# Second-layer products split into fp32r parts from chunk 7 on, with the third split product in steps 3 and 5 of a chunk

## The chip, the core and the metric

The kernel runs on one core of a Trainium2 chip. The metric is the device time of one execution in microseconds (us); the kernel before takes 1778.03 us, the median of three runs (1777.51 to 1778.36).

## What is computed

A Fourier mixing layer is followed by a two-layer block with the hard-swish activation:

```python
X = np.fft.fft(np.fft.fft(x, axis=1), axis=2).real      # x: 8 x 3008 x 256
x = X.reshape(24064, 256)
h = x @ w_in                                            # 256 x 2048
g = h * np.clip(h + 3.0, 0.0, 6.0) / 6.0
out = g @ w_out                                         # 2048 x 256
```

Inputs and output are float32.

## The kernel before

**Tiling.** The batch is four pairs (NP = 4). The sequence transform of a pair has two stages: `stage1` (64-row tables on TensorE, L327, copied out by L339 and L340 and sent to DRAM) and `stage2` (L563), which gives the transposed columns of one chunk. A pair has 12 chunks (NCK), 48 in all, numbered by `n_all`; a chunk is 256 columns wide, the last of each pair (`ch.last`) 192. The feature transform is folded into the first layer's weights. A chunk goes through the two layers in 8 steps (`fc`), each with 256 of the 2048 hidden features.

**First layer.** A *unit* is 512 columns of one step's hidden features. Its sums are split products: KQ and KW hold three fp32r parts of the data and of the weights, and a product is three fp32r matmuls (`passes`, L717). Even and odd rows of the contraction come apart: `passes(nx, 0)` adds the even rows of the next unit onto a seed that ScalarE wrote (`seed`, L732 and L736, from the row QN), ScalarE copies the even sum out (`keep_even`, L741, tile s), `odd_half` adds the odd rows (the 127-row matmuls of L717) and takes a relu of the sum (L791, t from u), VectorE forms the other sign (`other_sign`, L751, v in the PSUM tile y0), ScalarE takes its relu (L791, t from v), and two `gates` on VectorE (L794) write the activation A.

**Second layer.** Each step is seven Strassen products per chunk (`mlp2`, L865), accumulated in PSUM over the 8 steps. `combine` on GpSimd (L809) forms the four mixed operands c a step ahead. A plain product is one fp32 matmul, which the profile shows as two rows of L865. A *split product* is three fp32r matmuls: a high part with the weight kept in GH, and two others with the weights in GK. From chunk CHUNK2 = 8 on, NFR = 2 products of every step are split: `split_gates` makes the high part of two operands on ScalarE (L886), copies it into a PSUM tile y1 or y0 (L891) and lets VectorE make the other two (L892, L893, tile J). In steps listed in THIRD = (4,) a third product is split by `split_third` (L900 and L903 on ScalarE, L904 and L905 on VectorE), whose copy always goes to y0.

**Weights.** `split_weights` (L914 to L919) makes the parts GK, one step's weights at a time; `keep_high` (L924, L926) replaces a step's GH by its high part once no unsplit product needs it, through a PSUM bank: two ScalarE instructions.

**Order.** Everything is in program order per engine. The main loop (from L1689) runs one *cycle* per unit: `odd_half`, one product, `other_sign`, one product, even passes of the next unit, gates, then `size - 2 - behind_it` products, the matmuls of a `stage1` if there is one, and `behind_it` products; then the next seed, the high parts of a following step (`flush(high_of)`), and `third_others`. The numbers of products in each cycle come from `place`: 6 or 7 per cycle. With `sizes = [6] * 7 + [7] * 2` a chunk has nine cycles, with `[7] * 8` it has eight. `third_high` starts a third product's high part in the middle of a cycle, one step ahead; `third_others` at a cycle's end makes the rest. I count cycles from 1; chunk 3 has cycles 3 to 11, chunk 5 cycles 21 to 29 before, and chunk 8 starts with cycle 48.

Of the kernel before, what the change touches and what calls it, by code (L numbers as in the profile page):

```python
# [7 lines left out]
F32 = mybir.dt.float32  # L8
# [52 lines left out]
def kernel(  # L61
# [66 lines left out]
    NSLOT, CHUNK1 = 9, 3  # L128
    CHUNK2, NFR = 8, 2
    THIRD = (4,)  # L130
    SPLIT = CHUNK1 * NF - 2
# [5 lines left out]
    F1 = consts.tile([P, 5 * PB], F32, name="F1")  # L137
    FI = consts.tile([P, NIX + 1 + P], F32, name="FI")
    IX = FI[:, 0:NIX].bitcast(I32)
# [4 lines left out]
    G = consts.tile([P, 6 - NFR, NF, P], F32, name="G")  # L144

    def split_products(fc):
        return NFR + (fc in THIRD)

    GH = [consts.tile([P, split_products(fc), P], F32, tag=f"GH{fc}", name="GH") for fc in range(NF)]
    G2 = {fc: consts.tile([P, P], F32, tag=f"G2{fc}", name="G2") for fc in range(NF) if fc not in THIRD}  # L150

    def weight(i, fc):
        if i == NFR and fc in G2:
            return G2[fc][:]
        return GH[fc][:, i] if i <= NFR else G[:, i - NFR - 1, fc]
    half = consts.tile([P, 1], F32, name="half")
# [673 lines left out]
    def split_of(ch, fc):  # L830
        return ch.n_all >= CHUNK2

    def order_of(ch, fc):

        if not split_of(ch, fc):
            return [[(i, None)] for i in range(7)]
        high, others = ([(i, j) for i in range(NFR)] for j in (HIGH, OTHERS))
        rest = [[(i, ALL if i < split_products(fc) else None)] for i in range(NFR, 7)]
        if ch.final and fc >= NF - LAST:
            return [high, others] + [rest[i - NFR] for i in (3, 5, 6, 4, 2)]  # L840
        if fc in THIRD:
            rest = rest[1:3] + rest[0:1] + rest[3:]
        order = [high] + rest[:2] + [others] + rest[2:]
        while len(order) > 7:
            order[0:2] = [order[0] + order[1]]
        return order

    def mlp2(ch, fc, lo, hi):
        a = ch.a[fc].rearrange("p m f n -> p (m f) n")[:, :, 0:ch.n]
        c = ch.c[fc]  # L850
        moving = [a[:, 0], a[:, 1], a[:, 3], c[:, 0], c[:, 1], c[:, 2], c[:, 3]]
        order = order_of(ch, fc)
        if fc == NF - 1 and lo == 0:
            ch.e = epool.tile([P, 5, TB], F32, tag="e", bufs=1, name="e")
            if ch.final:
                ch.e2 = epool.tile([P, 2, TB], F32, tag="s", bufs=1, name="e")
        for i, parts in (x for part in order[lo:hi] for x in part):
            if fc == 0 and i % 2 == 0 and parts != OTHERS:
                ch.acc[i // 2] = ps_a.tile([P, 2, TB], F32, tag="acc", name="acc")
            o = ch.acc[i // 2][:, i % 2, 0:ch.n]  # L860
            for j in parts or (None,):
                assert (j is None) != (weight(i, fc).dtype == F32R)
                w = weight(i, fc) if not j else GK[fc][:, j - 1, i]
                x = moving[i] if j is None else J3[:, j, 0:ch.n] if i == NFR else parts_tile(ch, fc)[:, j, i, 0:ch.n]
                nc.tensor.matmul(o, w, x,  # L865
                                 start=(fc == 0 and i % 2 == 0 and j in (None, 0)), stop=(fc == NF - 1),
                                 skip_group_check=True)
# [42 lines left out]
    def split_weights(fc):  # L910

        low, rest = (GK[fc][:, k] for k in range(2))
        ps = bank([P, split_products(fc), P], "high")
        nc.scalar.mul(low, GH[fc][:], HIGH_PART)  # L914
        nc.vector.tensor_scalar(ps[:], low.bitcast(F32), 1.0 / EPS, None, op0=AL.mult)
        nc.vector.scalar_tensor_tensor(low, GH[fc][:], (1.0 + EPS) / EPS, ps[:], op0=AL.mult, op1=AL.subtract)
        nc.vector.scalar_tensor_tensor(ps[:], ps[:], -EPS, low.bitcast(F32), op0=AL.mult, op1=AL.add)
        yield
        nc.vector.tensor_scalar(rest, ps[:], 1.0 / (1.0 + EPS), None, op0=AL.mult)  # L919

    def keep_high(fc):

        ps = bank([P, split_products(fc), P], "high")
        nc.scalar.copy(ps[:], GH[fc][:])  # L924
        GH[fc] = consts.tile([P, split_products(fc), P], F32R, tag=f"GH{fc}", name="GH")
        nc.scalar.mul(GH[fc][:], ps[:], HIGH_PART)  # L926
        yield

# [173 lines left out]
    def join(j):  # L1102
# [7 lines left out]

        outs = GH[2 * n + i][:, 0:NFR], G[:, B12 - NFR - 1:B22 - NFR:B22 - B12, 2 * n + i]
        for h, o in enumerate(outs):
# [3 lines left out]
    def mix_w_out(j):  # L1116

        g = {i: G[:, i - NFR - 1, 2 * j:2 * j + 2, :] for i in range(NFR + 1, 7)}
        tt = nc.gpsimd.tensor_tensor
# [4 lines left out]
        for k in range(2):  # L1124
            tt(weight(2, 2 * j + k), g[5][:, k], GH[2 * j + k][:, B21], op=AL.subtract)

# [30 lines left out]


    def load_table():
        nc.sync.dma_start(out=F1[:], in_=c_stage1[:, 8 * PB:13 * PB])  # L1160
# [14 lines left out]
    load_w(0, nc.sync)  # L1175
    nc.scalar.dma_start(out=F[:], in_=c_stage1[:, 0:8 * PB])
    nc.scalar.dma_start(out=FI[:], in_=c_stage1[:, 13 * PB:])
    zero = QN[PB:PX, 2]
# [125 lines left out]
    def beside():  # L1304
# [5 lines left out]
        for t, gr in ((2, 2), (10, 3)):  # L1310
            put(t, load_t, gr)
        put(2, spread_half, halves[0], 1)
        put(5, load_table)
        put(NF - 1, close_w)
# [40 lines left out]
    def open_slots():  # L1355
        nonlocal A, GK
# [3 lines left out]
        GK = [slots.tile([P, 2, split_products(fc), P], F32R, tag=f"GK{fc}", name="GK") for fc in range(NF)]  # L1360

# [4 lines left out]

    epool = jpool = KW = A = GK = J = J3 = None
    steps = [(p, ck, fc) for p in range(NP) for ck in range(NCK) for fc in range(NF)]
# [256 lines left out]
    seed(units[1])  # L1625
    weights_of, rested, kept = list(range(NF)), 0, 0

# [3 lines left out]

    thirds = [s for s in gates_of if steps[s][2] in THIRD]
    third = []

    def third_high():

        if thirds and not third and thirds[0] <= now[0] + 1:
            ch, fc = chunk(thirds.pop(0))
# [50 lines left out]
    while done < len(stream):  # L1689
# [18 lines left out]
        third_high()  # L1708
        if not un:
            third_others()  # L1710

# [56 lines left out]
        flush(high_of)  # L1768
        third_others()
        for gen in parts:  # L1770
            next(gen, None)
# [112 lines left out]
```

## Time and profile before

| | |
|---|---|
| median of 3 runs | 1778.03 us |
| profiled execution, its own time | 1779.34 us |
| its span, first to last instruction | 1777.5 us |
| granted TensorE clock, mean | 0.999 |
| PE busy | 1764.3 us (99%) |
| VectorE (DVE) busy | 1494.5 us (84%) |
| ScalarE (ACT) busy | 1411.4 us (79%) |
| GpSimd (POOL) busy | 1312.7 us (74%) |

An execution's time is its span and 1.8 us around it. A busy time is a union of the instructions' durations. Matmuls overlap in the pipeline, so their durations (376 ns for a row of an fp32 matmul of 256 columns) are longer than the distances of their starts; a pace is read from starts, best from one cycle's first 127-row matmul of L717 to the next cycle's.

### The profile page before, as it was taken

The page shows a single profiled execution, that of the slowest core. Times are in us where ns is not written, and L with a number is a line of the kernel's source. Part 1 is how long each engine was busy: PE and PEld are TensorE (multiplying, and loading weights), DVE is VectorE, ACT ScalarE, POOL GpSimd, SP SyncE. Part 2 cuts the span into 40 slices and gives each one's busy share as a digit, 9 for nine tenths or more (in the row PEclk, how much of TensorE's full clock was granted, in tenths as well). Part 3 has the DMA queues.
Part 4 walks back from the last instruction along what each step waited for, and adds up shares of the span by engine and source line. Part 5 has one row for each costly group of instructions (what it writes and reads, how often), then busy time and mean ns, then how long its engine had stood idle before and what let it go on. Part 6 is the DMA issues. An engine that isn't in the chain of part 4 may idle for free.

```text
span 1777.5 us, 30218 instructions
## 1 busy us (share of the span) xinstructions
PE 1764.3 (99%) x9632; PEld 1518.3 (85%) x9632; DVE 1494.5 (84%) x2868; ACT 1411.4 (79%) x2573; POOL 1312.7 (74%) x1474
## 2 busy tenths in 40 slices
PE   8999999999999999999999999999999999999998
PEld 6688888888988888888998888888899888888897
DVE  8988676668988888888898888888899888888887
ACT  6556666678888888888888888888888888888885
POOL 5687777776678787886768878887766766776675
PEclk9999999999999999999999999999999999999999
DMA  8433332312113222121112222321111111101101
GB/s 281 121 93 99 103 78 70 85 37 51 37 48 81 71 64 78 47 73 43 30 44 64 70 78 57 86 64 37 48 36 34 37 21 48 41 19 45 21 13 34
DMA packets 160811, 110.39 MB, mean 62 GB/s; under 512 B 122562, under 2 KB 141344, under 8 KB 160652
## 3 DMA queue, kind: packets, MB, share of 16 engines
q1 hardware_dynamic: 151900, 82.22, 18.5%
q0 software_dynamic: 7504, 25.65, 4.7%
q8 instruction: 76, 1.25, 0.3%
q14 instruction: 83, 0.68, 0.1%
q10 hardware_dynamic: 1248, 0.59, 0.1%
HBM read 71.93 MB, written 36.79 MB: 61 GB/s over the span
## 4 chain that ended last, share of the span: by engine, by line
PE 95%; DVE 2%; ACT 2%; issue 0%; DMA 0%; another core or an unknown queue 0%; DVEq 0%; ACTq 0%
PE acc L865 58%; PE u L717 27%; PE ps L563 2%; PE ps L327 2%; PE acc L819 1%; PE v L613 1%; PE u L613 1%; ACT t L791 1%; PE spare L1138 0%; DVE v L751 0%; PE ps L526 0%; PE ps L395 0%; PE awake L1165 0%; DVE J L892 0%; ACT PM L1069 0%
## 5 line engine op out<-in xcount | busy, mean ns | idle before, releaser
L865 PE MATMUL acc<-c,G 128*128 128x256 f32 (+1 forms) x3008 | 766.7, 376 | 0.0
L717 PE MATMUL u<-KQ,KW 128*128 128x512 f32 (+7 forms) x2376 | 743.8, 426 | 1.0 <-ACT s L741 0.6
L809 POOL TENSOR_TENSOR c<-A 128x512 f32<-128x512 f32 (+1 forms) x359 | 453.9, 1264 | 337.3 <-PE acc L865 328.5
L865 PEld LDWEIGHTS acc<-c,G 128*128 128x128 f32 x3008 | 533.1, 189 | 80.3 <-issue 12.8
L717 PEld LDWEIGHTS u<-KQ,KW 128*128 128x128 f32 (+1 forms) x2376 | 426.1, 189 | 67.0 <-ACT s L741 3.0
L791 ACT ACTIVATE t<-u,half 128x512 f32<-128x512 f32 (+1 forms) x384 | 261.9, 682 | 169.9 <-PE u L717 111.7
L791 ACT ACTIVATE t<-v,half 128x512 f32<-128x512 f32 (+1 forms) x384 | 262.3, 683 | 106.1 <-DVE v L751 104.5
L751 DVE SCALAR_TENSOR_TENSOR v<-s,u 128x512 f32<-128x512 f32 (+1 forms) x360 | 247.0, 686 | 117.5 <-ACT t L791 111.6
L809 POOL TENSOR_TENSOR c<-c,A 128x256 f32<-128x256 f32 (+1 forms) x359 | 260.4, 725 | 28.2
L809 POOL TENSOR_TENSOR c<-A,c 128x256 f32<-128x256 f32 (+1 forms) x359 | 260.2, 725 | 28.2
L794 DVE SCALAR_TENSOR_TENSOR A<-t,v 128x512 f32<-128x512 f32 (+3 forms) x481 | 250.2, 541 | 36.7 <-ACT t L791 34.1
L865 PE MATMUL acc<-J,GK 128*128 128x256 f32 (+1 forms) x1340 | 270.7, 322 | 1.4 <-DVE J L905 0.8
L892 DVE SCALAR_TENSOR_TENSOR J<-high,A 128x512 fp32r<-128x512 f32 (+1 forms) x315 | 211.2, 670 | 55.8 <-ACT high L891 45.4
L794 DVE SCALAR_TENSOR_TENSOR A<-t,u 128x512 f32<-128x512 f32 (+3 forms) x481 | 248.4, 537 | 0.0
L732 ACT ACTIVATE u<-QN,WN 128x512 f32<-128x512 f32 (+1 forms) x324 | 224.8, 694 | 0.0
L865 PEld LDWEIGHTS acc<-J,GK 128*128 128x128 f32 x1340 | 204.7, 189 | 17.5 <-DVE J L893 1.6
L893 DVE SCALAR_TENSOR_TENSOR J<-high,A 128x512 fp32r<-128x512 f32 (+1 forms) x315 | 210.5, 668 | 0.0
L886 ACT ACTIVATE J<-A 128x512 fp32r<-128x512 f32 (+1 forms) x315 | 193.4, 614 | 0.0
L891 ACT COPY high<-J 128x512 f32<-128x512 f32 (+1 forms) x315 | 185.2, 588 | 4.9 <-DVE KQ L893 2.4
L741 ACT COPY s<-u 128x512 f32<-128x512 f32 (+2 forms) x315 | 180.3, 572 | 9.5 <-PE u L717 8.3
L865 PE MATMUL acc<-A,G 128*128 128x256 f32 (+1 forms) x630 | 184.6, 375 | 0.0
L865 PEld LDWEIGHTS acc<-J,GH 128*128 128x128 f32 x670 | 125.8, 189 | 24.1
(184 smaller groups left out, 1808.5 us busy)
## 6 DMA issues: line engine op xcount, KB each, us to landing
out_dram<-o SPq DMA_DIRECT2D x744, 32.0 KB
T<-in_c_stage_dram SPq DMA_DIRECT2D x26, 512.0 KB
g<-zd SPq DMA_DIRECT2D x42, 256.0 KB
zd<-z SPq DMA_DIRECT2D x48, 192.0 KB
QN<-qd SPq DMA_DIRECT2D x43, 128.0 KB
xt<-in_x_dram SPq DMA_DIRECT2D x21, 256.0 KB
st<-in_moe_w_out_dram POOLq DMA_DIRECT2D x7, 512.0 KB
xt<-in_x_dram SPq DMA_DIRECT2D x17, 192.0 KB
```

The costliest lines, as they stand in the source:

```text
L717: nc.tensor.matmul(un.wide(un.u[:]) if un.joint else un.u[:, i, 0:un.nq], un.weights(j, blk, i, rows), un.moving(j, blk, rows), start=Fals ...
L732: nc.scalar.activation(un.wide(un.u[:]), un.wide(row), AF.Identity, scale=WN[:, f:f + 1])
L741: copy(un.wide(un.s[:]), un.wide(un.u[:]))
L751: nc.vector.scalar_tensor_tensor(v, s, -2.0, u, op0=AL.mult, op1=AL.add)
L791: nc.scalar.activation(t, h, AF.Relu, bias=half[:], scale=scale)
L794: nc.vector.scalar_tensor_tensor(dst, t, 1.0, h, op0=AL.min, op1=AL.mult)
L809: (eng or nc.gpsimd).tensor_tensor(out, in0, in1, op=AL.add)
L865: nc.tensor.matmul(o, w, x, start=(fc == 0 and i % 2 == 0 and j in (None, 0)), stop=(fc == NF - 1), skip_group_check=True)
L886: nc.scalar.mul(high, a, 1.0 - EPS / 2.0)
L891: nc.scalar.copy(ps, high.bitcast(F32))
L892: nc.vector.scalar_tensor_tensor(low, ps, -1.0, a, op0=AL.mult, op1=AL.add)
L893: nc.vector.scalar_tensor_tensor(rest, ps, 1.0 + EPS, a, op0=AL.mult, op1=AL.subtract)
```

## The change

CHUNK2 goes from 8 to 7, so that chunk 7's two products a step are split too (16 more split products). THIRD goes from (4,) to (3, 5), without the last chunk of a pair: 74 third products of 256 columns in place of 36 of 256 and 4 of 192 columns.

Chunk 7 gets eight cycles in place of nine, and chunk 5 ten (six of 6 and four of 5 products), so that the number of cycles is the same. In all cycles before step 54 `behind_it` is 1, so that a stage1 comes one product later. `keep_high` moves from the middle of a cycle to its end, behind the seed and the thirds, with its scratch in y0, up to two in a cycle; `split_weights` may run every second cycle, and two more jobs split the third product's weights. `third_others` also starts a third product's high part. The row that is spread over the partitions is written into QN in place of a tile of its own, the index and sign columns are loaded a second time into a small tile (`load_index`, one DMA of 128 x 33 on SP), and the weights' tiles are cut differently.

```diff
-    CHUNK2, NFR = 8, 2
-    THIRD = (4,)
+    CHUNK2, NFR = 7, 2
+    THIRD = (3,5)
...
-        ch.row = qpool.tile([P, TB], F32, tag="row", name="row")
+        ch.row = QN[:, ch.n_all % 4]
...
+    def third_of(ch, fc):
+        return split_of(ch, fc) and fc in THIRD and not ch.last
...
+    def split_third_weights(fc):
+        yield from split_parts(weight(NFR, fc), bank([P, P], "high")[:], *(GK3[fc][:, j] for j in range(3)))
...
     def keep_high(fc):
-        ps = bank([P, split_products(fc), P], "high")
+        ps = ps_u.tile([P, NFR, P], F32, tag="y0", name="high")
         nc.scalar.copy(ps[:], GH[fc][:])
...
+    def load_index():
+        nonlocal FI, IX
+        FI, IX = signs, signs[:, 0:NIX].bitcast(I32)
+        nc.sync.dma_start(out=FI[:], in_=c_stage1[:, 13 * PB:13 * PB + NIX + 1])
...
-        sizes = [6] * 7 + [7] * 2 if n < CHUNK1 + 5 else [7] * 8
+        sizes = {5: [6] * 6 + [5] * 4}.get(n, [6] * 7 + [7] * 2) if n < CHUNK1 + 4 else [7] * 8
...
-    weights_of, rested, kept = list(range(NF)), 0, 0
+    weights_of = [(split_weights, fc) for fc in range(NF)] + [(split_third_weights, fc) for fc in THIRD]
+    rested, kept = 0, 0
...
     def third_others():
+        third_high()
         for gen in third:
             next(gen, None)
...
-        if kept < NF and not stages and not ends and done >= 7 * ((CHUNK2 - 1) * NF + kept - SPLIT) + 7:
-            splitting, kept = keep_high(kept), kept + 1
-            next(splitting)
-        elif weights_of and not stages and not ends and not closing and rested >= 3:
-            splitting, rested = split_weights(weights_of.pop(0)), 0
+        if weights_of and not stages and not ends and not closing and rested >= 2:
+            (f, fc), rested = weights_of.pop(0), 0
+            splitting = f(fc)
             next(splitting)
...
-        behind_it = 1 if any(s - 1 in middle_fns for s in begun) else 2
+        behind_it = 1 if any(s - 1 in middle_fns or s < CHUNK2 * NF - 2 for s in begun) else 2
...
         third_others()
+        for _ in range(2):
+            if kept < NF and not stages and not ends and done >= 7 * ((CHUNK2 - 1) * NF + kept - SPLIT) + NFR:
+                keep_high(kept)
+                kept += 1
```

**Where it moves instructions: ScalarE in a regular chunk.** First a piece of ScalarE's queue before, from cycle 99 to the start of cycle 100 (a pair's middle): t from u is the relu that opens a cycle, J from A 128x512 and 128x256 are the high parts of two products and of the third, s the copy of the even sums, u from QN the seed.

```order
L791 ACTIVATE t<-u,half 128x512
L886 ACTIVATE J<-A 128x512
L900 ACTIVATE J<-A 128x256
L791 ACTIVATE t<-v,half 128x512
L741 COPY s<-u 128x512
L891 COPY high<-J 128x512
L732 ACTIVATE u<-QN,WN 128x512
L903 COPY high<-J 128x256
L791 ACTIVATE t<-u,half 128x512
```

The same queue of the change, cycle 100 (cycle 98 reads the same, cycle 99 is without the two 128x256 rows) and the start of cycle 101, which holds the split of new columns KQ:

```order
L783 ACTIVATE t<-u,half 128x512
L884 ACTIVATE J<-A 128x512
L898 ACTIVATE J<-A 128x256
L783 ACTIVATE t<-v,half 128x512
L733 COPY s<-u 128x512
L889 COPY high<-J 128x512
L724 ACTIVATE u<-QN,WN 128x512
L901 COPY high<-J 128x256
L783 ACTIVATE t<-u,half 128x512
L884 ACTIVATE J<-A 128x512
```

The places within the cycle are the same; there are two such cycles in a chunk, 98 and 100, in place of one, 99.

**ScalarE where splitting begins.** Before, cycle 51 (in chunk 8) has the last `keep_high` (GH) ahead of the high copy, the seed and the third product's copy:

```order
L791 ACTIVATE t<-u,half 128x512
L886 ACTIVATE J<-A 128x512
L900 ACTIVATE J<-A 128x256
L791 ACTIVATE t<-v,half 128x512
L741 COPY s<-u 128x512
L924 COPY high<-GH 128x256
L926 ACTIVATE GH<-high 128x256
L891 COPY high<-J 128x512
L732 ACTIVATE u<-QN,WN 128x512
L903 COPY high<-J 128x256
```

In the change the last two `keep_high` stand in cycle 40, the first of chunk 7, behind the seed; six others are in cycles 31 to 37, which have no split products:

```order
L783 ACTIVATE t<-u,half 128x512
L884 ACTIVATE J<-A 128x512
L733 COPY s<-u 128x512
L783 ACTIVATE t<-v,half 128x512
L889 COPY high<-J 128x512
L724 ACTIVATE u<-QN,WN 128x512
L927 COPY high<-GH 128x256
L929 ACTIVATE GH<-high 128x256
L927 COPY high<-GH 128x256
L929 ACTIVATE GH<-high 128x256
```

So the eight ScalarE instructions of four `keep_high` that stood ahead of the seeds of cycles 48 to 51 are gone from there, and four instructions stand behind the seed of cycle 40.

**TensorE at an early stage1.** Before, cycle 4, from its even passes to the next cycle's odd passes (ps from y is stage1):

```order
L717 MATMUL u<-KQ,KW 128x256 x6
L865 MATMUL acc<-A,GH 128x256
L865 MATMUL acc<-A,G_112 128x256
L327 MATMUL ps_1871<-y,F_97 64x512
L327 MATMUL ps_1872<-y,F_97 64x512
L327 MATMUL ps_1871<-y,F_97 64x512
L327 MATMUL ps_1872<-y,F_97 64x512
L865 MATMUL acc<-c,G 128x256 x2
```

The same place in the change:

```order
L709 MATMUL u<-KQ,KW 128x256 x6
L863 MATMUL acc<-A,GH 128x256
L863 MATMUL acc<-A,G 128x256
L863 MATMUL acc<-c,G 128x256
L319 MATMUL ps_1860<-y,F_97 64x512
L319 MATMUL ps_1861<-y,F_97 64x512
L319 MATMUL ps_1860<-y,F_97 64x512
L319 MATMUL ps_1861<-y,F_97 64x512
L863 MATMUL acc<-c,G 128x256
```

One product has moved ahead of the stage1. The same holds in cycles 8, 14 and 22. The fifth early stage1 comes in cycle 28, one of the four cycles of 5 products, and has four products of its cycle ahead of it, as many as it had before in cycle 31.

More of the change, by code (lines that the diff above doesn't have):

```diff
@@ L143 @@
     WN = consts.tile([P, NFC], F32, name="WN")
[L144 to L150, printed above, removed]
+    G = consts.tile([P, 7 - NFR, NF, P], F32, name="G")
+    GH = [consts.tile([P, NFR, P], F32, tag=f"GH{fc}", name="GH") for fc in range(NF)]
     def weight(i, fc):
-        if i == NFR and fc in G2:
-            return G2[fc][:]
-        return GH[fc][:, i] if i <= NFR else G[:, i - NFR - 1, fc]
+        return GH[fc][:, i] if i < NFR else G[:, i - NFR, fc]
     half = consts.tile([P, 1], F32, name="half")
@@ L861, in mlp2 @@
             for j in parts or (None,):
-                assert (j is None) != (weight(i, fc).dtype == F32R)
-                w = weight(i, fc) if not j else GK[fc][:, j - 1, i]
-                x = moving[i] if j is None else J3[:, j, 0:ch.n] if i == NFR else parts_tile(ch, fc)[:, j, i, 0:ch.n]
+                w, x = weight(i, fc), moving[i]
+                if parts and i == NFR:
+                    w, x = GK3[fc][:, j], J3[:, j, 0:ch.n]
+                elif parts:
+                    w, x = GK[:, j - 1, fc, i] if j else w, parts_tile(ch, fc)[:, j, i, 0:ch.n]
+                assert (j is None) != (w.dtype == F32R)
                 nc.tensor.matmul(o, w, x,
@@ L1116, in mix_w_out @@
     def mix_w_out(j):
-        g = {i: G[:, i - NFR - 1, 2 * j:2 * j + 2, :] for i in range(NFR + 1, 7)}
+        g = {i: G[:, i - NFR, 2 * j:2 * j + 2, :] for i in range(NFR, 7)}
         tt = nc.gpsimd.tensor_tensor
@@ L1124, in mix_w_out @@
         for k in range(2):
-            tt(weight(2, 2 * j + k), g[5][:, k], GH[2 * j + k][:, B21], op=AL.subtract)
+            tt(g[2][:, k], g[5][:, k], GH[2 * j + k][:, B21], op=AL.subtract)
     def send_wn(f):
@@ L1176 @@
     nc.scalar.dma_start(out=F[:], in_=c_stage1[:, 0:8 * PB])
+    FI = wpool.tile([P, NIX + 1 + P], F32, name="FI")
+    IX = FI[:, 0:NIX].bitcast(I32)
     nc.scalar.dma_start(out=FI[:], in_=c_stage1[:, 13 * PB:])
@@ L1312, in beside @@
         put(2, spread_half, halves[0], 1)
+        put(2, load_index)
         put(5, load_table)
@@ L1359, in open_slots @@
         A = slots.tile([P, NSLOT, 2, 2, TB], F32, name="A")
-        GK = [slots.tile([P, 2, split_products(fc), P], F32R, tag=f"GK{fc}", name="GK") for fc in range(NF)]
+        GK = slots.tile([P, 2, NF, NFR, P], F32R, name="GK")
+        GK3 = {fc: slots.tile([P, 3, P], F32R, tag=f"GK{fc}", name="GK3") for fc in THIRD}
     def open_parts():
@@ L1625 @@
     seed(units[1])
-    weights_of, rested, kept = list(range(NF)), 0, 0
+    weights_of = [(split_weights, fc) for fc in range(NF)] + [(split_third_weights, fc) for fc in THIRD]
+    rested, kept = 0, 0
     def turn_before(s):
         return s - (3 if chunk(s)[0].final and steps[s][2] else 1)
-    thirds = [s for s in gates_of if steps[s][2] in THIRD]
+    thirds = [s for s in gates_of if third_of(*chunk(s))]
     third = []
@@ L1637, in third_high @@
         if thirds and not third and thirds[0] <= now[0] + 1:
+            assert thirds[0] > now[0]
             ch, fc = chunk(thirds.pop(0))
@@ L1708 @@
         third_high()
-        if not un:
-            third_others()
         swap = bool(un and nx and closing)
```

35 lines of the change are left out of this document (17 added, 18 removed).

## The prediction

> **What bounds the kernel now.** I read the page first: busy times, granted clock and the chain that ended last.
>
> ```profile
> PE 1764.3 (99%) x9632; PEld 1518.3 (85%) x9632; DVE 1494.5 (84%) x2868; ACT 1411.4 (79%) x2573; POOL 1312.7 (74%) x1474
> PEclk9999999999999999999999999999999999999999
> PE 95%; DVE 2%; ACT 2%; issue 0%; DMA 0%; another core or an unknown queue 0%; DVEq 0%; ACTq 0%
> ```
>
> TensorE is busy throughout at full clock, and the chain runs through it. A busy share can hide a slow pace, so I read the timeline next, TensorE alone, over three regular cycles (99 opens at 603.11, 100 at 607.37). Columns are start, time to the group's last end, operation, rows.
>
> ```profile
> 598.86 1.04 PE L717 MATMUL u<-KQ,KW 127*128 127x512 f32 x3
> ...
> 603.11 1.03 PE L717 MATMUL u<-KQ,KW 127*128 127x512 f32 x3
> ...
> 607.37 1.05 PE L717 MATMUL u<-KQ,KW 127*128 127x512 f32 x3
> ...
> 609.86 0.82 PE L865 MATMUL acc<-J,GK 128*128 128x256 f32 x4
> 610.51 0.28 PE L865 MATMUL acc<-J,GH 128*128 128x256 f32 x1
> 610.63 0.40 PE L865 MATMUL acc<-J,GK 128*128 128x256 f32 x2
> 610.87 1.02 PE L865 MATMUL acc<-c,G 128*128 128x256 f32 x4
> 611.54 1.05 PE L717 MATMUL u<-KQ,KW 127*128 127x512 f32 x3
> ...
> 613.79 1.05 PE L563 MATMUL ps<-T,g 128*128 128x128 f32 x8
> ```
>
> No row has a wait. Cycles 98 and 99 take 4.25 and 4.26 us; cycle 100, which uses the third product's parts that cycle 99 made, takes 4.17: one product split instead of whole saves 0.08 us. The rows agree: from 610.51 to 610.87 the three parts take 0.36, about 0.12 each. Where splitting begins there is a second reading:
>
> ```profile
> 374.67 1.05 PE L717 MATMUL u<-KQ,KW 127*128 127x512 f32 x3
> 379.08 1.05 PE L717 MATMUL u<-KQ,KW 127*128 127x512 f32 x3
> ```
>
> This cycle of seven whole products takes 4.41, 0.16 above 4.25 for five whole and two split ones: again 0.08 each. So TensorE's own stream sets the time, and what is left to gain is the stream's content and the few places where it stands.
>
> **The change, part by part**, against the profiled execution's 1779.34 us.
>
> *Streaming.* 16 products in chunk 7 and 74 - 36 = 38 third products of 256 columns are split anew: 54 x 0.08 = 4.3 us less. By rounding of the starts 0.07 to 0.09 each, 3.8 to 4.9. The four third products of 192 columns that become whole I put at nothing.
>
> The Trainium skill, in FP8 and Floating Point Precision, TensorE Precision Notes, has true fp32 as four passes through the array. By that rule three parts for four passes would save a quarter of a whole product, which by the rows is 0.36 + 0.08 = 0.44, so 0.11 apiece and 5.9 us in all. The cycles above show 0.08, and I keep that.
>
> *What must cover it.* A new third product costs these four rows, ScalarE's and VectorE's:
>
> ```profile
> L900 ACT ACTIVATE J<-A 128x256 fp32r<-128x256 f32 (+1 forms) x40 | 16.0, 399 | 0.0
> L903 ACT COPY high<-J 128x256 f32<-128x256 f32 (+1 forms) x40 | 14.7, 367 | 0.8 <-DVE J L893 0.7
> L904 DVE SCALAR_TENSOR_TENSOR J<-high,A 128x256 fp32r<-128x256 f32 (+1 forms) x40 | 16.3, 407 | 0.4 <-ACT high L903 0.4
> L905 DVE SCALAR_TENSOR_TENSOR J<-high,A 128x256 fp32r<-128x256 f32 (+1 forms) x40 | 16.3, 407 | 0.0
> 588.84:625.20 36.36, 36.36 (x195) 31.03 (x194) 31.23 (x56) 30.61 (x57) 29.74 (x33) 1.00 0.27 70
> ```
>
> That is 0.77 us on ScalarE and 0.81 on VectorE a chunk, and the last row, one chunk of 36.36 us, leaves VectorE 5.1 and ScalarE 5.7 idle. Cycle 99 has the same instructions in the same places today and TensorE doesn't wait there, so cycles 98 and 100 should not either: nothing, with up to 0.05 us a cycle (3.5 in all) as the bad end. The 16 gates of chunk 7's products run in chunk 8 today without a wait of their own.
>
> *Where splitting begins.* The starts of cycles 50 to 53, ScalarE's queue ahead of them, and last the relu that opens a regular cycle:
>
> ```profile
> 387.61 1.05 PE L717 MATMUL u<-KQ,KW 127*128 127x512 f32 x3
> 392.10 1.05 PE L717 MATMUL u<-KQ,KW 127*128 127x512 f32 x3
> 396.60 1.03 PE L717 MATMUL u<-KQ,KW 127*128 127x512 f32 x3
> 402.19 0.96 PE L717 MATMUL u<-KQ,KW 127*128 127x512 f32 x3 [0.63 <-ACT s L741]
> ```
> ```profile
> 387.32 0.39 ACT L924 COPY high<-GH 128x256 f32<-128x256 f32 x1
> 387.75 0.38 ACT L926 ACTIVATE GH<-high 128x256 fp32r<-128x256 f32 x1
> 388.03 0.59 ACT L891 COPY high<-J 128x512 f32<-128x512 f32 x1
> 388.54 0.69 ACT L732 ACTIVATE u<-QN,WN 128x512 f32<-128x512 f32 x1
> ...
> 398.98 0.38 ACT L903 COPY high<-J 128x256 f32<-128x256 f32 x1 [0.74 <-DVE J L893]
> ...
> 608.51 0.69 ACT L791 ACTIVATE t<-u,half 128x512 f32<-128x512 f32 x1 [0.32 <-PE u L717]
> ```
>
> Cycles of 4.49, 4.50 and 5.59 where 4.25, 4.25 and 4.17 would do: 1.9 us lost, because keep_high puts 0.71 us (387.32 to 388.03) ahead of a seed, and in the queue of cycle 51 the third copy and the high copy share one PSUM tile. In the change six keep_high lie in cycles 31 to 37, whose ScalarE queue has no split products in it, so this loss goes: -1.9, at worst moved and not gone, 0. Late next is ScalarE in cycle 40 with two keep_high behind its seed: 1.42 us, of which a cycle's idle time before the opening relu takes 0.3 (the last row) and the lead of the copy s before TensorE's next odd rows 0.6 (the rows under collisions: 903.46 to 904.12). I take +0.5, between 0 and 1.4.
>
> *Last chunks.* Cycles 75 and 76 of the trace's first pair, the second with a third product of 192 columns:
>
> ```profile
> 497.55 0.96 PE L717 MATMUL u<-KQ,KW 127*128 127x512 f32 x3
> 501.26 0.96 PE L717 MATMUL u<-KQ,KW 127*128 127x512 f32 x3
> 505.36 0.97 PE L717 MATMUL u<-KQ,KW 127*128 127x512 f32 x3
> ```
>
> 4.10 against 3.71: here ScalarE and VectorE are the bound and the third product costs 0.39. It goes in three pairs: -1.2. In the fourth, the kernel's end, it holds up TensorE once:
>
> ```profile
> 1764.28 0.47 PE L865 MATMUL acc<-J,GK 128*128 128x192 f32 x2 [0.84 <-DVE J L905]
> ```
>
> I take -0.7, between 0 and -0.9, since GpSimd's operands are not far behind.
>
> *Early stage1.* Its weight loads wait for VectorE's second gate, which frees y0:
>
> ```profile
>   DVE A L794: 2.8, 5
> ```
>
> 2.8 us in five places. In four of them one more whole product (0.43) now comes first: -1.7; the fifth, in cycle 28, keeps its wait. Ends 0 and -2.1.
>
> *Collisions.* In cycles 68, 164 and 260 the third product of step 5 meets the split of new columns, and its copy needs the PSUM tile that the high copy holds until L893 ends. The rows there today:
>
> ```profile
> 900.61 0.68 DVE L893 SCALAR_TENSOR_TENSOR J<-high,A 128x512 fp32r<-128x512 f32 x1
> 900.93 0.59 ACT L791 ACTIVATE t<-u,half 128x388 f32<-128x388 f32 x1 [0.34 <-PE u L717]
> 902.88 0.58 ACT L741 COPY s<-u 128x512 f32<-128x512 f32 x1
> 904.12 1.03 PE L717 MATMUL u<-KQ,KW 127*128 127x512 f32 x3
> ```
>
> The copy can start at 901.29 and ends 0.37 later, so the relu of 900.93 and, in its train, the copy s, which ends at 903.46, come 0.7 to 0.9 late: 0.1 to 0.3 past TensorE's need at 904.12, with the handover 0.35. Three times: +1.0, at worst 2.7.
>
> *Short cycles.* In the four cycles of five products TensorE needs 0.43 less than today. ScalarE there:
>
> ```profile
> 273.48 1.00 ACT L736 ACTIVATE u<-QN,WN 128x256 f32<-128x256 f32 x2
> 274.95 0.69 ACT L791 ACTIVATE t<-u,half 128x512 f32<-128x512 f32 x1 [0.47 <-PE u L717]
> ```
>
> It waits 0.47 for TensorE and would wait 0.04: just enough, so +0.4 for the four, up to 1.2.
>
> *At nothing:* load_index (one more small DMA on SP in step 2; behind it stand table and column loads that are wanted steps later, and the gathers of step 5 wait for it), the row in QN (the same copies, with a DMA wait less), more frequent split_weights, all in cycles without split gates on VectorE, GpSimd's folds, which move a cycle against its additions at 74% busy. If a cover were missing, each would show as one wait of under a microsecond.
>
> Sum: -4.3 - 1.9 - 1.2 - 0.7 - 1.7 + 0.5 + 1.0 + 0.4 = -7.9 us, so 1771.4 for a profiled execution. The median of the runs stands 1.3 us below the profiled one; the same step gives 1778.03 - 7.9 = **1770.1**.
>
> **Rivals.** *The stalls only move.* Everything around the stream is repaid elsewhere (cycle 40, the collisions, the short cycles at their bad ends) and the streaming gain stays: 1774 to 1775. For it: ScalarE's reserves are 0.3 and 0.6 us, and two keep_high are 1.42. Against it: the third products leave the last chunks for good.
>
> *ScalarE becomes the bound in step 5's cycle.* Place: the copy L903 of the second third product in every chunk, behind a seed and ahead of the opening relu. Where it is as late as in cycle 76, a chunk loses 0.39 at its price there: 37 x 0.39 = 14.4, so 1778.0 - 7.9 + 14.4 = 1784.5, slower. It decides from 7.9 / 37 = 0.21 us a chunk on. For it: two more instructions, 0.77 us, against a reserve of 0.3 in front of the relu. Against it: cycle 99 has the same queue and TensorE stands nowhere; cycle 101, behind the new one, holds a stage2 (613.79, about 1 us), which gives the queue time.
>
> *Four passes.* If a split product saves a quarter of a whole one after all, 54 x 0.11 = 5.9 and the time is 1768.5; the 4.25 and 4.17 of the cycles speak against it. It is the rule of the Trainium skill's page above.
>
> **How the numbers follow.** A difference of 0.2%, 3.6 us, is about what a measurement of this kernel can tell from no change: faster is below 1774.5. My forecast has 0.65, the stalls that move 0.20 (half of it faster, half within 0.2%), ScalarE's bound 0.10 (0.08 slower, 0.02 within), four passes 0.05. So faster 0.65 + 0.05 + 0.10 = 0.80, the same 0.10 + 0.02 = 0.12, slower 0.08. Good ends of all terms (-4.9 - 1.9 - 1.2 - 0.9 - 2.1) give 1767.0, four passes a microsecond less; the bad ends of the additions on the streaming gain (-4.3 - 1.2 + 1.4 + 2.7 + 1.2, and half of 3.5) give about 1779.6, which need not all meet. I take 1766 to 1776, which leaves out the slower case.
>
> **What would show it.** L865's fp32 rows fall by 2 x 50, its fp32r rows rise by 150. Cycles 99 and 101 use the third products and take 0.08 less than today, without a wait. The cycles of chunk 8 without thirds take 4.25, none 4.5; the last chunks' cycles of 192 columns take 3.7, none 4.1. The stage1 waits on L794 fall from 2.8 to about 1.1. I am wrong if cycles behind 100 grow, if cycles 164 and 165 lose over 1 us, or if those of 5 products take 4 us.

## The result, and the profile after

The changed kernel takes **1770.59 us** (median of 6 runs, 1768.85 to 1771.63) where the kernel before took 1778.07 in the runs beside it (1777.03 to 1778.36): ratio 0.9957, 95% interval 0.9946 to 0.9969, or 7.5 us less. The forecast was 1770.1. The profiled execution took 1769.10, its span 1767.3. One execution of experiment 4's kernel took 3530.71 us at a granted clock of 0.94 and is left out of its ratio.

The page of the changed kernel, the lines that answer to those of before: busy times and the chain.

```profile
PE 1757.2 (99%) x9682; PEld 1516.3 (86%) x9682; DVE 1523.7 (86%) x2960; ACT 1438.4 (81%) x2659; POOL 1311.2 (74%) x1474
...
PE 97%; DMA 1%; DVE 1%; ACT 1%; issue 0%; POOL 0%; DVEq 0%; POOLq 0%; ACTq 0%
```

TensorE is still the bound, with 97% of the chain. VectorE has 29 us more to do and ScalarE 27, and TensorE is busy for 7 us less. Its instructions grow from 9632 to 9682: 150 fp32r rows more, 2 x 50 fp32 rows less.

The timeline of the changed kernel, the rows that open cycles 98 to 103 (start, time to the group's last end):

```profile
592.66 1.05 PE L709 MATMUL u<-KQ,KW 127*128 127x512 f32 x3
...
596.91 1.03 PE L709 MATMUL u<-KQ,KW 127*128 127x512 f32 x3
...
601.09 1.05 PE L709 MATMUL u<-KQ,KW 127*128 127x512 f32 x3
...
605.34 1.03 PE L709 MATMUL u<-KQ,KW 127*128 127x512 f32 x3
...
610.41 1.05 PE L709 MATMUL u<-KQ,KW 127*128 127x512 f32 x3
...
614.66 1.03 PE L709 MATMUL u<-KQ,KW 127*128 127x512 f32 x3
```

From start to start: 4.25, 4.18, 4.25, 5.07 (with its stage2), 4.25. Cycles 99 and 101 use the third products; before they took 4.26 and 5.15. The cycles beside them have not grown, though ScalarE and VectorE now do the third product's work twice a chunk.

Where splitting had stalled, the rows that open cycles 50 to 53:

```profile
384.11 1.05 PE L709 MATMUL u<-KQ,KW 127*128 127x512 f32 x3
...
388.36 1.03 PE L709 MATMUL u<-KQ,KW 127*128 127x512 f32 x3
...
392.54 1.05 PE L709 MATMUL u<-KQ,KW 127*128 127x512 f32 x3
...
396.79 1.03 PE L709 MATMUL u<-KQ,KW 127*128 127x512 f32 x3
```

4.25, 4.18, 4.25 where it was 4.49, 4.50, 5.59. And where splitting now begins, the openings of cycles 40 to 42:

```profile
338.76 1.05 PE L709 MATMUL u<-KQ,KW 127*128 127x512 f32 x3
...
343.04 1.05 PE L709 MATMUL u<-KQ,KW 127*128 127x512 f32 x3
...
347.60 0.97 PE L709 MATMUL u<-KQ,KW 127*128 127x512 f32 x3
```

Cycle 40 takes 4.28; cycle 41 takes 4.56, 0.31 too much, behind the two keep_high of cycle 40. Cycle 46, with a stage1, takes 5.93 and is looked at below.

I read every cycle's start in both traces. Of the 10.1 us by which the last cycle's last matmul starts earlier, 1.75 lie before cycle 1, whose opening rows are, before and after:

```profile
167.32 1.07 PE L717 MATMUL u<-KQ,KW 127*128 127x256 f32 x6
```

```profile
165.56 1.07 PE L709 MATMUL u<-KQ,KW 127*128 127x256 f32 x6
```

That is not the change: the same opening code started cycle 1 anywhere from 165.6 to 167.5 in the twelve profiles of the changed kernel and its variants, and at 167.3 and 166.4 in two profiles of the opening of before. So I compare cycles 1 to 360 alone, from the opening of cycle 1 to TensorE's last matmul. Most cycles repeat to a few hundredths from profile to profile, where medians move by a microsecond with the opening. The change takes 8.35 us off them; 7.9 were forecast.

### The profile page after: what moved, and what is told of

Read it like the earlier page. It is cut to its first block, busy times and chain, and to the rows that moved or that the text cites. A ratio compares the mean times of both kernels' runs of the same rounds, so it can differ in the third digit from the quotient of the medians.

```text
span 1767.3 us, 30553 instructions
## 1 busy us (share of the span) xinstructions
PE 1757.2 (99%) x9682; PEld 1516.3 (86%) x9682; DVE 1523.7 (86%) x2960; ACT 1438.4 (81%) x2659; POOL 1311.2 (74%) x1474
## 4 chain that ended last, share of the span: by engine, by line
PE 97%; DMA 1%; DVE 1%; ACT 1%; issue 0%; POOL 0%; DVEq 0%; POOLq 0%; ACTq 0%
PE acc L863 60%; PE u L709 28%; PE ps L555 2%; PE ps L319 2%; PE acc L811 1%; PE v L605 1%; PE u L605 1%; PE spare L1140 0%; DMA xt<-in_x_dram,IT 0%; ACT PM L1071 0%; PE ps L518 0%; DMA st<-in_moe_w_in_dram 0%; POOL xt L208 0%; PE ps L425 0%; DMA g<-z 0%
## 5 line engine op out<-in xcount | busy, mean ns | idle before, releaser
L863 PE MATMUL acc<-J,GK 128*128 128x256 f32 (+1 forms) x1514 | 289.6, 319 | 0.5 <-DVE J L891 0.5
L890 DVE SCALAR_TENSOR_TENSOR J<-high,A 128x512 fp32r<-128x512 f32 (+1 forms) x323 | 216.3, 670 | 54.9 <-ACT high L889 49.1
L863 PEld LDWEIGHTS acc<-J,GK 128*128 128x128 f32 x1514 | 223.5, 189 | 17.1 <-DVE J L891 1.4
L891 DVE SCALAR_TENSOR_TENSOR J<-high,A 128x512 fp32r<-128x512 f32 (+1 forms) x323 | 215.4, 667 | 0.0
L884 ACT ACTIVATE J<-A 128x512 fp32r<-128x512 f32 (+1 forms) x323 | 198.2, 614 | 0.0
L889 ACT COPY high<-J 128x512 f32<-128x512 f32 (+1 forms) x323 | 190.3, 589 | 5.9 <-DVE KQ L891 3.1
L863 PE MATMUL acc<-A,G 128*128 128x256 f32 (+1 forms) x572 | 167.0, 374 | 0.0
L863 PEld LDWEIGHTS acc<-J,GH 128*128 128x128 f32 x646 | 121.3, 189 | 24.4
```

The lines of the kernel that those rows point to most:

```text
L863: nc.tensor.matmul(o, w, x, start=(fc == 0 and i % 2 == 0 and j in (None, 0)), stop=(fc == NF - 1), skip_group_check=True)
L884: nc.scalar.mul(high, a, 1.0 - EPS / 2.0)
L889: nc.scalar.copy(ps, high.bitcast(F32))
L890: nc.vector.scalar_tensor_tensor(low, ps, -1.0, a, op0=AL.mult, op1=AL.add)
L891: nc.vector.scalar_tensor_tensor(rest, ps, 1.0 + EPS, a, op0=AL.mult, op1=AL.subtract)
```

## The experiments

"More" and "less" mean cycles 1 to 360 of one profile against the changed kernel's, unless said otherwise; the medians stand beside them, each with its ratio to before.

**1. No third product.**

```diff
-    THIRD = (3,5)
+    THIRD = ()
```

> The change without any third split product (THIRD empty); everything else as in the change. My theory, TensorE's stream sets the time and a split product of 256 columns saves 0.08 us: 74 x 0.08 = 5.9 us more than the change, about 1776.5, and cycles 99 and 101 take 4.25 and 5.15 in place of 4.18 and 5.07. Four passes against three (0.11 apiece): 8.1 more, about 1778.7. ScalarE as a hidden bound in the cycles with a third copy: clearly less than 5.9 more, 3 or below, and cycles next to the thirds' get shorter when the thirds go.

Measured: 1775.61 us (0.9988, 0.9978 to 0.9998); in the cycles 5.8 us more, 0.079 for each of the 74. The openings of cycles 99 to 102:

```profile
599.09 1.05 PE L709 MATMUL u<-KQ,KW 127*128 127x512 f32 x3
...
603.35 1.03 PE L709 MATMUL u<-KQ,KW 127*128 127x512 f32 x3
...
607.60 1.05 PE L709 MATMUL u<-KQ,KW 127*128 127x512 f32 x3
...
612.75 1.03 PE L709 MATMUL u<-KQ,KW 127*128 127x512 f32 x3
```

Cycles 99 and 101 take 4.26 and 5.15, as in before. Only cycle 46 became shorter without thirds (5.76 for 5.93); no regular cycle did. The stream's price stands, 0.11 apiece falls, and no hidden bound on ScalarE shows.

**2. Thirds in the last chunks too.**

```diff
-        return split_of(ch, fc) and fc in THIRD and not ch.last
+        return split_of(ch, fc) and fc in THIRD
```

> The change with third split products also in the last chunks (steps 3 and 5, 192 columns). My theory, in narrow cycles ScalarE and VectorE are the bound and a third product costs 0.39 there: cycles 75, 171 and 267 take 4.1 in place of 3.71; the second one falls in a cycle with a stage2 (77, 173, 269), which gives the queues time and stays at 4.62; the tail gets 0.5 back. 3 x 0.39 + 0.5 = 1.7 us more than the change. Rival, the third costs the same wherever it stands in these chunks: 6 x 0.39 + 0.5 = 2.8 more. Rival, the 0.39 belonged to step 4's place alone: within 0.3 of the change.

Measured: 1773.02 us (0.9976, 0.9966 to 0.9985); 3.5 us more. The openings of cycles 75 to 79:

```profile
492.19 0.95 PE L709 MATMUL u<-KQ,KW 127*128 127x512 f32 x3
...
496.28 0.97 PE L709 MATMUL u<-KQ,KW 127*128 127x512 f32 x3
...
500.01 0.96 PE L709 MATMUL u<-KQ,KW 127*128 127x512 f32 x3
...
504.64 1.00 PE L709 MATMUL u<-KQ,KW 127*128 127x256 f32 x6
...
508.92 0.97 PE L709 MATMUL u<-KQ,KW 127*128 127x512 f32 x3
```

Cycle 75 takes 4.09 (3.71 in the change), 77 stays at 4.63, but 78, behind it, takes 4.28 in place of 3.93. Both thirds cost 0.35 to 0.39, so the first rival is right: the loss comes a cycle behind the stage2. The last cycle, the tail, takes 0.70 more; the rest is two single regular cycles (235 and 323), 0.29 and 0.14 longer, which I leave open.

**3. The early stage1 one product earlier again.**

```diff
-        behind_it = 1 if any(s - 1 in middle_fns or s < CHUNK2 * NF - 2 for s in begun) else 2
+        behind_it = 1 if any(s - 1 in middle_fns for s in begun) else 2
```

> The change with stage1 one product earlier again in the early cycles, as before (two products behind it instead of one). My theory, the stage1's weight loads wait for the second gate: cycles 4, 8 and 22 are 0.44 longer again and cycle 28 up to 0.4, together 1.3 to 1.7 us more than the change. Rival, those cycles became shorter through the other edits: no difference in them, within 0.2 us in all.

Measured: 1771.72 us (0.9962, 0.9948 to 0.9976); 1.4 us more. Cycles 4, 8 and 22 take 0.44, 0.43 and 0.43 more, and nothing else moves, cycle 28 included. The weight loads in cycle 4, as in before, wait 0.83 for the second gate between the first two and the rest:

```profile
185.62 0.20 PEld L319 LDWEIGHTS ps<-y,F 47*64 47x64 f32 x6 [0.83 <-DVE A L786]
```

In the changed kernel the same place shows 0.39.

**4. The kernel before with keep_high at cycles' ends, nothing else.**

```diff
-        ps = bank([P, split_products(fc), P], "high")
+        ps = ps_u.tile([P, split_products(fc), P], F32, tag="y0", name="high")
...
-        if kept < NF and not stages and not ends and done >= 7 * ((CHUNK2 - 1) * NF + kept - SPLIT) + 7:
...
         third_others()
+        for _ in range(2):
+            if kept < NF and not stages and not ends and done >= 7 * ((CHUNK2 - 1) * NF + kept - SPLIT) + 3:
+                keep_high(kept)
+                kept += 1
```

> The kernel before with one edit alone: keep_high at the end of a cycle, behind the seed, in y0, up to two a cycle; they fall in cycles 39 to 42, two in 45 and two in 48 (before: 40, 41, 43, 45 and 48 to 51). My theory, keep_high ahead of the seeds caused the loss of 1.9 us in cycles 50 to 52: it goes (4.25, 4.25, 4.17), and each pair in one cycle costs about 0.3 in the cycle behind it: 1.2 to 1.3 us less than before. Rival, the loss came from the first third product and the start of the split gates, not from keep_high: cycles 50 to 52 stay at 4.5, 4.5 and 5.6 and the time stays within 0.5 us of before or grows by the pairs.

Measured: 1777.57 us (0.9997, 0.9987 to 1.0006); against the cycles of before 1.0 us less. The openings of cycles 49 to 53:

```profile
383.11 1.03 PE L717 MATMUL u<-KQ,KW 127*128 127x512 f32 x3
...
387.68 0.96 PE L717 MATMUL u<-KQ,KW 127*128 127x512 f32 x3
...
391.86 1.05 PE L717 MATMUL u<-KQ,KW 127*128 127x512 f32 x3
...
396.12 1.03 PE L717 MATMUL u<-KQ,KW 127*128 127x512 f32 x3
...
400.29 1.05 PE L717 MATMUL u<-KQ,KW 127*128 127x512 f32 x3
```

Cycles 50 to 52 take 4.18, 4.26 and 4.17: the whole loss of 1.9 goes with this edit alone, the first third product (cycle 52) included. The pairs cost 0.32 in cycle 49 (4.57), as expected, and 0.73 in cycle 46 (6.35 for 5.62), more than expected, since a stage1 stands there. So where the edit puts keep_high decides, and half of its gain is lost again in this kernel. (The edit also moves keep_high's scratch from y1 to y0; no run takes the place and the tile apart.)

**5. One product behind every stage1, one keep_high a cycle.**

```diff
-        behind_it = 1 if any(s - 1 in middle_fns or s < CHUNK2 * NF - 2 for s in begun) else 2
+        behind_it = 1
...
-        for _ in range(2):
+        for _ in range(1):
             if kept < NF and ...
```

> The change with one product behind every stage1 (not only the early ones) and one keep_high a cycle (cycles 40 and 41, not two in 40). In the change's trace the 14 stage1 of four matmul pairs from cycle 89 on stand 1.32 us where cycle 38's takes 1.02, because the second gate frees y0 0.3 late; the two big ones stand 1.77 against 1.63. My theory, the product comes first and hides this, and cycle 41 loses its 0.3: 14 x 0.3 + 2 x 0.14 + 0.3 = 4.8 us less than the change, about 1766. Rival, stage1's copies on ScalarE then end later and hold up the relu and the copy s of the next cycle: the cycles 90, 98, 106 grow by 0.3 or more and the time stays, or grows.

Measured: 1770.62 us (0.9959, 0.9945 to 0.9972), the change's time; 0.55 us more. Cycle 41 lost its 0.31, as forecast for the pair (cycle 42 gave 0.09 back). Every late stage1 cycle became 0.30 shorter (97: 5.48 for 5.78), the next 0.11 longer and the one after 0.30 longer (99: 4.48 for 4.18). The weight loads of the odd rows, by what they waited for, in the change and in this run:

```profile
PEld u L709 <- ACT s L733: 1.5, 6, 0.4
```

```profile
PEld u L709 <- ACT s L733: 10.0, 35, 0.4
```

So the rival's outcome, a cycle later than it said: stage1's copies end later on ScalarE, and the two instructions of the third product of step 3, two cycles behind the stage1, keep its queue late until the copy s, for which TensorE waits 0.41 at the end of cycle 99. Run 12 tests this.

**6. Thirds in neighbouring steps.**

```diff
-    THIRD = (3,5)
+    THIRD = (4,5)
```

> The change with the third split product in steps 4 and 5, next to each other, in place of 3 and 5: as many split products, but the second one's high part and copy then come together at a cycle's end. My theory, ScalarE has 0.3 us in front of the opening relu and 0.6 ahead of the copy s, and 0.77 come at once: cycle 101 or 102 (and so in each of 37 chunks) loses 0.1 to 0.4, 4 to 15 us more than the change. Rival, the stage2 of cycle 101 and the free time over a chunk (5.7 us) take it up: within 0.5 us of the change.

Measured: 1775.56 us (0.999, 0.9981 to 0.9999); 5.7 us more. In most chunks cycle 102 takes 4.40 to 4.46 in place of 4.25, in the chunks 10, 22 and 34 two cycles each take 0.3 more, and cycles 46 and 54 take 0.46 and 0.31 more. ScalarE ahead of cycle 101's relu, and its relu and copy s in cycle 102:

```profile
607.26 0.71 ACT L724 ACTIVATE u<-QN,WN 128x512 f32<-128x512 f32 x1
607.88 0.42 ACT L898 ACTIVATE J<-A 128x256 fp32r<-128x256 f32 x1
608.33 0.38 ACT L901 COPY high<-J 128x256 f32<-128x256 f32 x1
608.64 0.68 ACT L783 ACTIVATE t<-u,half 128x512 f32<-128x512 f32 x1
...
615.41 0.69 ACT L783 ACTIVATE t<-v,half 128x512 f32<-128x512 f32 x1 [0.70 <-DVE v L743]
616.00 0.58 ACT L733 COPY s<-u 128x512 f32<-128x512 f32 x1
```

Both of the third's instructions stand between seed and relu, and the relu starts 1.51 behind its cycle's opening (607.13), where in the change it is 1.13. In cycle 102 ScalarE then waits 0.70 for VectorE's other sign, and the copy s ends at 616.58, right before the odd rows at 616.63, for which TensorE waited. A bound like that of the prediction's second rival thus exists, at 0.16 a chunk, with VectorE's queue as a part of it; with the thirds two steps apart it isn't reached.

**7. Chunk 7 whole.**

```diff
-    CHUNK2, NFR = 7, 2
+    CHUNK2, NFR = 8, 2
```

(with `s < 54` in place of `s < CHUNK2 * NF - 2`, which is the same step)

> The change with chunk 7 whole again (CHUNK2 = 8; the sizes of chunks 5 and 7, THIRD and the stage1 places of the change kept); keep_high then falls in cycles 40, 41, 43 (two), 44, 46 (two) and 48. My theory, 18 split products of chunk 7 are worth 18 x 0.08 = 1.4 us, and two keep_high in a cycle cost 0.3 in the next where a stage1 or split gates follow, while the 0.3 of cycle 41 and the loss of 0.15 to 0.45 in cycle 46 (column parts and split gates on VectorE ahead of the gates) go: 1.0 to 1.6 us more than the change. Rival, splitting chunk 7 gives back what it gains: within 0.4 us of the change.

Measured: 1770.5 us (0.996, 0.9945 to 0.9975); 1.2 us more, of which 0.28 are in the single cycle 75, which has no part in the edit. So splitting chunk 7, with the keep_high that move with it, is worth about 1.0 us in the cycles, and 18 split products alone would be 1.4; the medians, 0.1 apart, can't tell it.

**8 to 11. Where else the thirds could stand, with the edits of 5.** One line each, in this order:

```diff
-    THIRD = (3,5)
+    THIRD = (4,6)
+    THIRD = (4,7)
+    THIRD = (5,7)
+    THIRD = (1,5)
```

> One product behind every stage1, one keep_high a cycle, and the third split products in steps 4 and 6 (cycles 100 and 102) in place of 3 and 5. In the run with steps 3 and 5 the 0.30 that a stage1 cycle (97) gained came back as a wait for the copy s at the end of cycle 99, where the third product's two ScalarE instructions met a queue still late from stage1's copies. My theory, without a third product there the queue catches up within cycles 98 and 99 and the gain stays: 16 x 0.30 + 0.3 for cycle 41 = 5.1 us less than the change in the cycles, less up to 0.1 a chunk where step 6's parts meet the column parts around cycle 101. Rival, the delay is carried to the next third product: cycle 100 grows by 0.3 and no more than 0.5 is gained.

> As the run with steps 4 and 6, with steps 4 and 7 (cycles 100 and 103). My theory as there, 5.1 us less than the change; step 7's parts come in cycle 102, behind the column parts, whose VectorE half is in its queue: cycle 102 or 103 may lose 0.1 to 0.3 in 37 chunks (4 to 11 us), which would be more than the gain. Rival, no loss there: 5 us less than the change.

> As the run with steps 4 and 6, with steps 5 and 7 (cycles 101 and 103). My theory, 5.1 us less than the change if the queue has caught up by cycle 100, since the first third product comes one cycle later still; step 7 as in the run with steps 4 and 7: up to 0.3 lost in cycle 102 or 103 of each chunk. Rival, the delay is carried on to cycle 101: nothing gained.

> One product behind every stage1, one keep_high a cycle, and the third split products in steps 1 and 5 (cycles 97 and 101): none in the two cycles behind a stage1, none in 102 and 103, which lost time in the runs with steps 6 and 7. My theory, a stage1 is worth 0.30 in its own cycle less 0.11 in the next, 16 times, and 0.3 in cycle 41: 3.3 us less than the change. Rival, step 1's parts come in cycle 96, whose queues on ScalarE and VectorE are full with the end of a chunk: the gates of cycle 97 come later, stage1 waits for them again, and cycles 96 and 97 lose 0.2 to 0.4 in 37 chunks, 7 to 15 us, so slower than before the change or equal.

Measured: 1776.43 us (0.999, 0.998 to 0.9999), 1775.89 (0.9989, 0.9979 to 0.9998), 1781.35 (1.0022, 1.0012 to 1.0032) and 1774.75 (0.9982, 0.9973 to 0.9991); in the cycles 6.9, 6.8, 12.0 and 5.1 us more. In all four my sum was wrong. One half held in the first three: with no third in cycle 99 the 0.30 of cycle 97 stays, less 0.11 in cycle 98. But with steps 4 and 6, cycle 102 takes 4.56 for 4.25. ScalarE there, and the rows that open cycles 102 and 103:

```profile
614.38 0.38 ACT L901 COPY high<-J 128x256 f32<-128x256 f32 x1 [0.79 <-DVE J L891]
...
616.98 0.58 ACT L733 COPY s<-u 128x512 f32<-128x512 f32 x1
```

```profile
613.05 1.03 PE L709 MATMUL u<-KQ,KW 127*128 127x512 f32 x3
...
617.61 0.96 PE L709 MATMUL u<-KQ,KW 127*128 127x512 f32 x3
```

Step 6's copy meets the split of the new columns in every chunk: it waits 0.79 for the PSUM tile, and s ends at 617.56, 0.26 behind the time at which the odd rows of the next cycle would have opened after 4.25 (617.30). This is the collision that the prediction priced, now at its full 0.3, where I had allowed 0.1. Step 7 costs 0.86 in cycles 47 and 55 in both runs; with steps 5 and 7 it also costs 0.49 in cycle 63 and 0.21 in cycle 103 and its like, with steps 4 and 7 only 0.05 there; and the last cycle takes 0.7 more in both, which I had not foreseen. With steps 1 and 5 the rival came true for the stage1: its weight loads wait for the second gate again (0.21 in cycle 97), and cycle 97 takes 5.79, so nothing of the 0.30 is gained. Step 1 also costs 0.8 in cycle 41 and 0.2 to 0.4 in the cycles 49, 57 and 65 and some like them, though only a part of the chunks pays.

**12. Step 3's third left out only behind a late stage1.** The edits of 5, and

```diff
-        return split_of(ch, fc) and fc in THIRD and not ch.last
+        return split_of(ch, fc) and fc in THIRD and not ch.last and not (fc == 3 and (13 <= ch.n_all <= 20 or 25 <= ch.n_all <= 32))
```

> The change with one product behind every stage1, one keep_high a cycle, and step 3's third product left whole in the 16 chunks with a late stage1 (chunks 13 to 20 and 25 to 32); steps 3 and 5 in all others. My theory, each of these chunks gains 0.30 in the stage1's cycle, gives back 0.11 in the next and loses 0.08 of streaming in cycle 99: 16 x 0.11 = 1.8 us, and 0.3 in cycle 41, together 2.1 us less than the change in the cycles. Rival, the delay waits for the next third product (step 5, cycle 101) and costs 0.3 there: 16 x 0.08 = 1.3 us more than the change.

Measured: **1766.87 us** (5 runs, 1765.64 to 1767.86; 0.9935, 0.9922 to 0.9949), below every run of the change; 3.3 us less in the cycles. The openings of cycles 97 to 100:

```profile
587.68 1.03 PE L709 MATMUL u<-KQ,KW 127*128 127x512 f32 x3
...
593.16 1.05 PE L709 MATMUL u<-KQ,KW 127*128 127x512 f32 x3
...
597.52 0.96 PE L709 MATMUL u<-KQ,KW 127*128 127x512 f32 x3
...
601.68 1.03 PE L709 MATMUL u<-KQ,KW 127*128 127x512 f32 x3
```

5.48, 4.36, 4.16, against 5.78, 4.25, 4.18. Cycle 99 has one split product less and is no longer for it: its three opening matmuls take 0.96, not 1.03, behind the wait. So a chunk gains 0.20 and not 0.11. Sixteen split products fewer and a faster kernel: the place was worth more than the product.

## Why the prediction was right, point by point

The likeliest case happened, and the time came within half a microsecond. Two terms had the wrong size, in opposite directions, and two small ones were not foreseen. So the half microsecond is in part luck: the collisions came 0.9 cheaper, and the early stage1 0.3 and cycle 46 0.6 dearer. The profiled executions, whose openings differ, are 10.2 us apart, the cycles 8.35 and the medians 7.5.

| term | forecast | cycles 1 to 360 |
|---|---|---|
| streaming | -4.3 | -4.60 (what the other rows leave of 8.35) |
| stall of cycles 50 to 52 (53 with them) | -1.9 | -1.82 |
| last chunks (76, 172, 268) | -1.2 | -1.17 |
| tail (last cycle) | -0.7 | -0.53 |
| early stage1 (4, 8, 22; 28 for 31) | -1.7 | -1.40 |
| two keep_high (41, 42) | +0.5 | +0.23 |
| collisions (behind 68, 164, 260) | +1.0 | +0.06 |
| short cycles (27, 29, 30) | +0.4 | +0.48 |
| not foreseen: stage1 in a split cycle (46 to 48) | | +0.58 |
| not foreseen: cycle 19 | | -0.18 |

*Streaming* was right, and run 1 gives it by itself: 5.8 us for 74 products, so 4.3 for 54. The rule that I weighed, true fp32 as four passes (the Trainium skill, FP8 and Floating Point Precision, TensorE Precision Notes), would make that an estimated 74 x 0.11 = 8.1; the measured 0.079 a product doesn't bear out a quarter.

*The stall* was right in size and cause; run 4 shows it with keep_high's move alone. *The last chunks* were right; run 2 shows that the price is paid wherever the third product stands there.

*Early stage1* was the step that failed in its count. I took four places, and the section on the change names cycle 14 with the others; but cycle 14 had one product behind its stage1 before already, and it takes 5.73 in both traces. Three gained 0.43 to 0.44 (run 3), and cycle 28 is 0.09 shorter than cycle 31 was after the 0.43 of its missing product. So the waits on the second gate did not fall to 1.1 but from 2.8 to 2.4, with a new one in cycle 46:

```profile
PEld ps L319 <- DVE A L786: 2.4, 7, 0.4
```

*Collisions* were the term most off. ScalarE around cycle 165 of the changed kernel:

```profile
894.01 0.38 ACT L901 COPY high<-J 128x256 f32<-128x256 f32 x1 [0.73 <-DVE J L891]
894.42 0.59 ACT L783 ACTIVATE t<-u,half 128x388 f32<-128x388 f32 x1
...
896.43 0.57 ACT L733 COPY s<-u 128x512 f32<-128x512 f32 x1
```

The copy waits 0.73 for the PSUM tile, as I said, but it starts only 1.02 behind the cycle's opening (892.99). The relu comes 0.39 late (1.43 behind the opening, where it was 1.04) and the copy s 0.45 (3.44 for 2.99), not 0.7 to 0.9. It ends at 897.00, and the odd rows open at 897.15 in time. The step that failed here was to take the end of the split gate from the rows of before: there it ends 1.40 behind the opening (901.29), in a queue that holds step 4's third product a cycle earlier. The change moves that third to step 3, and the gate ends 0.99 behind, as it does without any third (0.98 in run 1). Run 6, with a third in step 4 again, shows the forecast price; its cycle 165 opens at 895.69:

```profile
896.38 0.68 DVE L891 SCALAR_TENSOR_TENSOR J<-high,A 128x512 fp32r<-128x512 f32 x1
```

```profile
897.56 0.59 ACT L783 ACTIVATE t<-u,half 128x388 f32<-128x388 f32 x1
...
899.51 0.58 ACT L733 COPY s<-u 128x512 f32<-128x512 f32 x1
```

There the gate ends 1.37 behind the opening, relu and s both start 0.83 later than in before, and cycle 165 takes 4.45 where the change has 4.16. So the mechanism and its size were right for that queue, and the queue was not the changed kernel's.

*Cycle 46* I had not seen. Seven whole products and a stage1 took 5.62; with two of them split it takes 5.93, where the stream alone would give 5.46. VectorE's queue in it:

```profile
366.12 0.68 DVE L891 SCALAR_TENSOR_TENSOR J<-high,A 128x512 fp32r<-128x512 f32 x1
366.71 0.68 DVE L644 SCALAR_TENSOR_TENSOR KQ<-ps,KQ 128x512 fp32r<-128x512 f32 x1
...
367.91 0.68 DVE L647 SCALAR_TENSOR_TENSOR KQ<-KQ,ps 128x512 fp32r<-128x512 f32 x1
...
369.10 0.68 DVE L786 SCALAR_TENSOR_TENSOR A<-t,v 128x512 f32<-128x512 f32 x1
```

The split gates, which end at 366.80 (L891), and the parts of new columns (L644, L647) stand ahead of the gates; the second gate starts at 369.10, ends at 369.78, and the stage1 that started at 369.36 waits for it. Of the 5.93, 0.17 belong to the third product, for run 1 has 5.76 here. I had put the split gates of chunk 7 at nothing because they ran in chunk 8 without a wait, and had not looked at the stage1 that they would stand ahead of here.

*Short cycles* cost what was forecast. TensorE's wait there is for the copy s, 0.24, 0.23 and 0.24 us at the ends of cycles 27, 29 and 30.

*Cycle 19*'s 0.18 goes with the more frequent split_weights, which I had put at nothing. In before a weight split's last VectorE instruction (L919) ends at 252.24, and the first matmul of the cycle's stage2 (L526) starts at 252.29, 2.55 behind the opening; in the change no weight split stands there, and it starts 2.47 behind. Run 4, which keeps the splits where they were, keeps the cycle at 5.52, and every run with the change's splits has 5.34. No run tests this alone, and by which wait the split held up the stage2 is not shown.

## What to carry to other kernels

Price a place, not a product: the same third split product saved 0.08 us in most cycles, cost 0.35 to 0.39 in the narrow ones, and cost more than it saved two cycles behind a stage1, beside the new columns' parts, or next to another third. Where one engine streams without a gap, a queue on another has so many tenths of reserve in each cycle; a delay is carried through the cycles until one with room, so look two cycles on before you count a gain. Where a change moves an instruction, time its neighbours in the changed order and not in today's: the collision of cycle 165 was priced in a queue that the change itself emptied. Compare cycle starts where the opening of a run moves its time by more than the edit does.

## What the runs showed of the hardware that was not expected

The first 165 us differ by up to 1.9 us between executions of the same opening (165.6 to 167.5), and nearly every cycle behind repeats to a few hundredths of a microsecond; in before's trace one of TensorE's first waits is put by the profile to no engine of the core:

```profile
PE awake L1165 <- remote: 2.2, 1, 2.2
```

No other trace here has that wait, though they differ among themselves by those 1.9 us, so it is at most a part of it. Behind a short wait TensorE's three opening matmuls take 0.96 in place of 1.03 to 1.05, so that 0.07 to 0.09 of a wait come back in the cycle behind it (cycle 42 at 4.17 behind 41, cycle 99 at 4.16 in run 12).
